# A convolution and MLP kernel whose exponential sums are kept and range-checked, with a looped general version behind a branch

## The chip, the cores and the metric

The kernel runs on one core of one Trainium2 chip. A core has five engines that run their own instruction lists and meet through semaphores: TensorE (PE in the profile; its weight loads are PEld), VectorE (DVE), ScalarE (ACT), GpSimd (POOL) and SyncE (SP), which here only issues DMAs. The metric is the device time of one execution in microseconds, lower is better.

## The reference

A dynamic convolution over seven taps, weighted by a softmax, followed by an MLP with the activation h - tanh(h):

```python
batch, seq, d_model = (8, 4096, 192); kernel_size = 7; n_heads = 8
...
w = weight_gen - np.max(weight_gen, axis=-1, keepdims=True)
w = np.exp(w)
w = w / (np.sum(w, axis=-1, keepdims=True) + 1e-09)
x_pad = np.concatenate([np.zeros((B, pad, D), dtype=np.float32), x], axis=1)
...
out = np.einsum('bshk,bskhg->bshg', w, x_unf)
...
h = x @ w_in
g = h - np.tanh(h)
return (g @ w_out).astype(np.float32)
```

`x` is drawn as 0.1 times a standard normal, `weight_gen` as 0.3 times one, `moe_w_in` and `moe_w_out` as normals over the square root of their first dimension.

## The kernel before

The 32,768 tokens are cut into 32 blocks (`NTOT`) of 1024 tokens (`TOK` = 128 partitions x `J` = 8). Everything is unrolled in Python; there is no loop or branch on the chip. A block `n` goes through these stages, several blocks being under way at once:

- `load_wg` and `load_x` (lines 116 and 126) fetch the tap weights and the tokens with their halo, on SyncE's queue.
- `softmax_exp` (167, ScalarE), `softmax_sum` (179, VectorE, in two halves of 32 columns), then the reciprocal (`softmax_norm`, 194; `softmax_recip`, 189) and the scaling (`scale`, 228). The kernel before takes exp of the raw weights, without subtracting the row maximum. Each block's 64 sums per partition live in a tile `zsum` of the pool `wgpool`, which has three buffers.
- `products` and `help` (261 and 243) multiply tokens and weights on GpSimd and VectorE; DMAs with accumulation sum some of the taps (`dma_sum`, 235).
- `conv_sums` and `conv_out` (367 and 395) sum the rest and transpose on TensorE into `convT`.
- `gemm1(n, f)` (422) makes, for each of 16 tiles `f` of the 2048 hidden columns, six matmuls into a PSUM tile `ph`; ScalarE takes tanh into `th` (line 440), VectorE subtracts into `gt` (line 441). `ph` comes from a PSUM pool with three buffers, which the transposes (`pc`) and the last block's outputs (`po2`) share.
- `out_stream` and `out_pairs` (481 and 525) feed the second matmul of earlier blocks between the first matmuls of this one, by hand-written counts (`STEADY`, 682, and others); `store_out` (508) copies a finished token tile out of PSUM and stores a block once its eight tiles are there.

The order on every engine is the order of the Python calls, as the whole body stands under `tc.manual_schedule()` (line 564). The main loop (707 to 768) runs `n` = 1 to 31 and `f` = 0 to 15. The exp of block `n + 4` is taken at f=1 of block `n`, its sums at f=1 and f=13, its reciprocal and scaling at f=14; from `n` = 28 on there is no such block.

After the loop comes the tail (770 to 774): the first half of `gemm2_last(0)`, the rest of `out_stream`, the second half, and then `gemm2_last(j)` (line 529) for the token tiles j = 1 to 7 of the last block. Each makes 32 matmuls into a `po2` tile, a ScalarE copy `ot` (551) and a VectorE add into `out_sb` (552). After every odd `j` SyncE stores two token tiles (554). The program then ends with a wait for all DMAs and a barrier of the engines, which the profile books under line 800.

Of the kernel before, what the change touches and what calls it, by code (L numbers as in the profile page):

```python
# [8 lines left out]
FP32 = mybir.dt.float32  # L9
BF16 = mybir.dt.bfloat16  # L10

ACT = mybir.ActivationFunctionType
AX = mybir.AxisListType


@with_exitstack
def kernel(
# [20 lines left out]
    JH = J // 2  # L38
    HT = TOK // 2
    NSB = S // TOK  # L40
    NTOT = B * NSB
    NFT = F // P
    NC = D // R
# [7 lines left out]
    HELP = {n: ((n - 2, 3),) for n in (4, 5, 6, 7, 8, 9, 10, 11, 12, 13, 14, 15, 16, 17, 18, 19, 20, 21, 22, 23, 24, 25, 26, 27, 28, 29, 30, 31)} | {9: ((7, 3), (6, 12)), 10: ((8, 3), (7, 12)), 11: ((9, 3), (8, 12)), 12: ((10, 3), (9, 12)), 13: ((11, 3), (10, 12)), 14: ((12, 3), (11, 12))}  # L51
    LAST_TAP = (4, 5, 6, 7, 8)
    X_LATE = ()
    ZERO_AT = 8
    PACE, PACED = None, ()
    SCALE_TWICE = True
# [24 lines left out]
    zero = const.tile([1, D], FP32, name="zero")  # L81
    nc.vector.memzero(zero[:])
    once = const.tile([P, 1], FP32, name="once")

    x_of = {}
    held = {}
# [2 lines left out]
    zsum_of = {}  # L89
    zr_of = {}  # L90
    wsm_of = {}
    prods_of = {}
    to_sum = {}
    conv_of = {}
# [99 lines left out]
    def softmax_norm(n, bank):  # L194

        wsm = softmax_tile()
        zr_v = bank[:, 512 - J * H : 512]
        nc.vector.reciprocal(zr_v, zsum_of[n][:])  # L198

        def finish():  # L200
            scale(nc.vector, wsm[:], e_of[n], zr_v)

        wsm_of[n] = (wsm, None, None, None)
        return finish

    def softmax_norm_ramp(n, bank):

        softmax_sum(n)
        wsm = softmax_tile()
        zr_v = bank[:, 512 - J * H : 512]  # L210
        nc.vector.reciprocal(zr_v, zsum_of[n][:])  # L211
# [14 lines left out]
        wsm_of[n] = (wsm, wsm_v, None, None)  # L226
# [298 lines left out]
    def out_pairs(m):  # L525
        for _ in range(m):
            next(pairs)

    def gemm2_last(j, f0=0, f1=NFT):
# [21 lines left out]
        nc.scalar.activation(out=ot[:], in_=po[:, 0, 0:D], func=ACT.Copy)  # L551
        nc.vector.tensor_add(out_sb[:, j, :], po[:, 1, 0:D], ot[:])
        if j % 2 == 1:
            nc.sync.dma_start(
                out=out[n * TOK : (n + 1) * TOK, :].rearrange("(p j) e -> p j e", p=P)[
                    :, j - 1 : j + 1, :
                ],
                in_=out_sb[:, j - 1 : j + 1, :],
            )
# [147 lines left out]
    for n in range(1, NTOT):  # L707
        more = n < NTOT - 1
        finish = []
        plan = FIRST if n == 1 else DOUBLE if n in DOUBLE_IN else APART if n in APART_IN else STEADY  # L710

        soft = [m for m in (n + 3 if n <= AHEAD else n + 4,) if m < NTOT]
        for f in range(NFT):
            ph = gemm1(n, f)
            if n == 1:
                if f == 1:
                    load_wg(5)
                if f == 5:
                    softmax_exp(4)
                steps = ((softmax_sum, 3), (softmax_recip, 3), (softmax_sum, 4))  # L720
                for at, (step, m, h) in zip(plan["sums"], [s + (h,) for s in steps for h in (0, 1)]):
                    if f == at:
                        step(m, h * JH, (h + 1) * JH)
                if f == 5:
                    wsm_of[3] = (softmax_tile(), None, e_of[3], zr_of[3])
                    rest = products(3)
            elif f == 1:
                if soft:
                    softmax_exp(soft[0])
                if n + 2 < NTOT:  # L730
                    rest = products(n + 2)
            if n == AHEAD and f == 4:
                softmax_exp(n + 4)
            if n > 1:
                for h, at in enumerate(plan["sums"]):
                    if soft and f == at:
                        softmax_sum(soft[0], h * JH, (h + 1) * JH)
            if n == AHEAD:
                for at, (step, h) in zip(EXTRA, [(s, h) for s in (softmax_sum, softmax_recip) for h in (0, 1)]):
                    if f == at:  # L740
                        step(n + 4, h * JH, (h + 1) * JH)
                if f == EXTRA[-1]:
                    wsm_of[n + 4] = (softmax_tile(), None, e_of[n + 4], zr_of[n + 4])
            for m in (n + 2, n + 3):
                if (n, f) in HELP.get(m, ()):
                    help(m, ph, J - 1 - HELP[m].index((n, f)))
            if n + 2 < NTOT and f == (9 if n == 1 else max([b for a, b in HELP.get(n + 2, ()) if a == n] + [3])):
                rest()
            if f == (9 if n == 1 else 1) and n > STORE_FIRST:
                loads(n)  # L750
            done = 0
            for chunks, at in sorted((((0, 1), plan["t2"]), ((2,), plan["t1"])), key=lambda c: c[1]):
                if more and at[0] == f:
                    out_pairs(at[1] - done)
# [12 lines left out]
            if f == (9 if n == 1 else 1) and n <= STORE_FIRST:  # L767
                loads(n)

    gemm2_last(0, 0, J)  # L770
    out_pairs(NFT)
    gemm2_last(0, J, NFT)
    for j in range(1, J):
        gemm2_last(j)


# [28 lines left out]
```

## Time and profile before

| What | Value |
|---|---|
| timed runs | 746.78 us median of 3 (745.8 to 747.22) |
| span of the profiled execution, which is a run of its own | 743.4 us |
| busy share: TensorE, its weight loads, VectorE, ScalarE, GpSimd | 97%, 75%, 92%, 86%, 88% |
| matmuls into `ph` (L427) | 3072, 415.1 us |
| second matmuls into `obank` (L495) | 7936, 408.0 us |
| subtractions `gt` (L441) | 512, 601.6 us, 1217 ns each |
| tanh `th` (L440) | 512, 512.1 us, 1025 ns each |
| sums `zsum` (L183) | 61, 23.6 us |
| final stores (L554) | 4 of 192 KB, 3.0 us from issue to landing (median) |

A group's busy time is the sum of its instructions' durations; matmuls overlap, so their sum can exceed the span. The idle time that the profile lists before an instruction is how long its engine did nothing, and the releaser is what it waited for. The chain of waits goes back from the last instruction to what released each one.

### The profile page before, as it was taken

Reading aid. Unit: us, or ns where it says so; the run is one execution under the profiler, and the core shown is the slowest. Engines: PE = TensorE matmul, PEld = TensorE weight load, DVE = VectorE, ACT = ScalarE, POOL = GpSimd, SP = SyncE. Lnnn points to the kernel's source line nnn. Section 1 sums busy time; section 2 is a strip of 40 time slices with the busy share of each in tenths; the row PEclk is TensorE's granted clock in tenths of the full one; section 3 lists DMA queues with packets and bytes.
Section 4 is the critical chain, followed back from the end, with each engine's and each line's share of the span. In section 5 each row is a group of like instructions: output and inputs, shape, how many; then the busy total and the mean of one; then the engine's idle time right before and its main releaser. Section 6 shows DMA issues by size and latency. Waiting matters only on the chain.

```text
span 743.4 us, 30037 instructions
## 1 busy us (share of the span) xinstructions
PE 722.3 (97%) x13616; PEld 556.5 (75%) x13616; DVE 687.4 (92%) x723; ACT 638.8 (86%) x872; POOL 654.5 (88%) x163
## 2 busy tenths in 40 slices
PE   3899999999999999999999999999999999999997
PEld 2477777778777777777777777777777777877777
DVE  7999899999999999999999999999999999988893
ACT  4888888888888888989889999898998989888882
POOL 7999999999999999999999999999999999991000
PEclk9899999999999999999999999999999999999999
DMA  8925367766567668878777977877887877776112
GB/s 236 245 46 161 135 172 185 195 179 149 124 183 184 183 185 224 210 199 203 166 202 209 236 186 204 178 195 205 221 209 195 192 181 194 193 149 110 45 45 86
DMA packets 34269, 130.06 MB, mean 175 GB/s; under 512 B 4591, under 2 KB 9439, under 8 KB 30174
## 3 DMA queue, kind: packets, MB, share of 16 engines
q0 software_dynamic: 19424, 51.12, 40.4%
q1 hardware_dynamic: 14718, 77.03, 27.6%
q8 instruction: 106, 1.74, 0.9%
q14 instruction: 21, 0.17, 0.1%
HBM read 54.52 MB, written 25.17 MB: 107 GB/s over the span
## 4 chain that ended last, share of the span: by engine, by line
PE 92%; DVE 5%; ACT 1%; issue 1%; DMA 1%; SPq 0%; DVEq 0%
PE ph L427 43%; PE obank L495 43%; PE pc L384 4%; DVE gt L441 3%; PE po L538 1%; ACT th L440 1%; DVE pa L299 1%; DMA wg_t<-in_weight_gen_dram 1%; DVE zsum L183 0%; SPq L134 0%; ACT convT L402 0%; DVE obank L211 0%; DVE pa L251 0%; DVE pb L299 0%; SPq L144 0%
## 5 line engine op out<-in xcount | busy, mean ns | idle before, releaser
L441 DVE TENSOR_TENSOR gt<-ph,th 128x1024 bf16<-128x1024 f32 x512 | 601.6, 1217 | 33.4 <-ACT th L440 23.2
L440 ACT ACTIVATE th<-ph 128x1024 f32<-128x1024 f32 x512 | 512.1, 1025 | 69.2 <-PE ph L427 60.3
L427 PE MATMUL ph<-convT,w_in 64*128 64x512 bf16 x3072 | 415.1, 379 | 5.3 <-DVE gt L441 3.3
L495 PEld LDWEIGHTS <-gt 64*128 64x128 bf16 x7936 | 355.6, 94 | 80.6 <-issue 6.3
L495 PE MATMUL obank<-w_out,gt 64*128 64x192 bf16 x7936 | 408.0, 243 | 0.9 <-issue 0.8
L299 POOL TENSOR_TENSOR pa<-x_t,wsm 128x2688 bf16<-128x2688 f32 (+3 forms) x68 | 338.9, 5232 | 0.2
L299 POOL TENSOR_TENSOR pb<-x_t,wsm 128x4608 bf16<-128x4608 f32 (+2 forms) x33 | 283.8, 8601 | 0.7 <-ACT wsm L221 0.5
L427 PEld LDWEIGHTS <-w_in 64*128 64x128 bf16 x3072 | 163.0, 94 | 86.0 <-issue 18.3
L514 ACT ACTIVATE out_sb<-obank 128x192 f32<-128x192 f32 x248 | 81.3, 328 | 11.2 <-PE obank L495 10.3
L410 ACT ACTIVATE convT<-pc 128x1024 bf16<-128x1024 f32 (+1 forms) x62 | 50.1, 810 | 2.9 <-PE pc L384 2.7
L236 POOL DMA_DIRECT2D pa<-pb x28 | 36.0, 1284 | 13.7 <-POOL pb L299 9.1
L384 PEld LDWEIGHTS <-pa 64*128 64x128 bf16 x2064 | 41.5, 100 | 6.8 <-DVE pa L299 1.1
L236 POOL DMA_DIRECT2D pa<-pa x21 | 34.7, 1651 | 9.6 <-DMA pa<-pb 8.9
L384 PE MATMUL pc<-ident,pa 64*128 64x64 bf16 x1968 | 41.2, 191 | 1.8 <-POOL pa L299 0.9
L183 DVE TENSOR_REDUCE zsum<-wg_t 128x32 f32<-128x224 f32 (+1 forms) x61 | 23.6, 387 | 2.9 <-ACT wg_t L169 2.9
L169 ACT ACTIVATE wg_t<-wg_t 128x448 f32<-128x448 f32 x32 | 18.2, 570 | 6.3 <-DMA wg_t<-in_weight_gen_dram 6.2
L251 DVE TENSOR_TENSOR pa<-x_t,ph 128x384 bf16<-128x384 f32 x34 | 18.8, 554 | 2.0 <-DVE ph L250 0.3
L229 DVE TENSOR_TENSOR wsm<-wg_t,pc 128x448 f32<-128x448 f32 x27 | 16.8, 621 | 2.5
L198 DVE RECIPROCAL pc<-zsum 128x64 f32<-128x64 f32 x27 | 14.9, 550 | 0.0
L384 PE MATMUL pc<-ident,pb 64*128 64x64 bf16 x216 | 4.9, 206 | 9.0 <-POOL pb L299 9.0
L384 PEld LDWEIGHTS <-pb 64*128 64x128 bf16 x288 | 6.3, 106 | 9.5 <-POOL pb L299 9.0
L538 PE MATMUL po<-w_out,gt 64*128 64x192 bf16 x256 | 11.2, 243 | 0.0
(27 smaller groups left out, 56.8 us busy)
## 6 DMA issues: line engine op xcount, KB each, us to landing
x_t<-in_x_dram SPq DMA_DIRECT2D x31, 1344.0 KB, 7.9
pa<-pb POOLq DMA_DIRECT2D x28, 1152.0 KB, 9.5
out_dram<-out_sb SPq DMA_DIRECT2D x31, 768.0 KB, 3.9
pa<-pa POOLq DMA_DIRECT2D x21, 768.0 KB, 7.2
wg_t<-in_weight_gen_dram SPq DMA_DIRECT2D x32, 224.0 KB, 7.1
x_t<-in_x_dram SPq DMA_DIRECT2D x1, 768.0 KB
w_out<-in_moe_w_out_dram POOLq DMA_DIRECT2D x1, 768.0 KB, 9.5
out_dram<-out_sb SPq DMA_DIRECT2D x4, 192.0 KB, 3.0
```

The source lines that it names most:

```text
L183: nc.vector.reduce_sum(out=zsum_of[n][:, j0 * H : j1 * H], in_=e_of[n][:, j0:j1].rearrange("p j h k -> p (j h) k"), axis=AX.X,)
L236: return nc.gpsimd.dma_start(out=out.rearrange("p k j d -> p k (j d)"), in_=in_.rearrange("p k j d -> p k (j d)"), accum_op=mybir.AluOpTyp ...
L251: nc.vector.tensor_mul(pa[:, 0:KH, j, :].rearrange("p k (h g) -> p k h g", h=H), bass.AP(tensor=x_v.tensor, offset=x_v.offset + j * D, ap= ...
L299: return eng.tensor_mul(prod(k0, k1)[:, :, j0:j1].rearrange("p k j (h g) -> p k (j h) g", h=H), bass.AP(tensor=x_v.tensor, offset=x_v.offs ...
L384: nc.tensor.matmul(pc[r][:, col : col + R] if home else pc[:, r, col : col + R], lhsT=prods[c][gi][r * R : (r + 1) * R, 2 * j : 2 * j + 2] ...
L410: last_conv[0] = nc.scalar.activation(out=out, in_=pc[:, :, 0:cols].rearrange("p r (cj t) -> p r cj t", t=R), func=ACT.Copy,)
L427: nc.tensor.matmul(ph[:, r, :], lhsT=w_in[r * R : (r + 1) * R, c, f * P : (f + 1) * P], rhs=convT[r * R : (r + 1) * R, c, :], start=(c == ...
L440: last_act[0] = nc.scalar.activation(out=th[:], in_=ph_f, func=ACT.Tanh)
L441: last_sub[0] = nc.vector.tensor_sub(gt[:], ph_f, th[:])
L495: mm = nc.tensor.matmul(po[:, 0:D], lhsT=g_of[n][f][r * R : (r + 1) * R, col : col + P], rhs=w_out[r * R : (r + 1) * R, f, :], start=(r == ...
L514: last_act[0] = nc.scalar.activation(out=out_sb[:, j, :], in_=po[:, 0:D], func=ACT.Copy)
L538: nc.tensor.matmul(po[:, r, 0:D], lhsT=g_of[n][f][r * R : (r + 1) * R, col : col + P], rhs=w_out[r * R : (r + 1) * R, f, :], start=(f == 0 ...
```

## The change

The sums of exponentials of all blocks are written side by side into one tile `zall` (128 x 2048) instead of into `zsum` buffers, and they are checked: their largest value must be at most 1e30 and their smallest at least 1e-18. The check is cut into eight pieces. Pieces 0 to 3 are reductions over halves of `zall`: the maximum of the first and second half at (n, f) = (28, 14) and (29, 14), the minimum of the first and second half at (30, 14) and (31, 8). After the loop, pieces 4 and 5 compare, piece 6 multiplies and moves the result of all partitions into one row by a DMA, and piece 7, ahead of token tile 4, reduces that row to one flag.

The flag is then loaded into a register of every engine, and where it is 0 the engines run a general version: loops on the chip over batch rows, blocks and hidden tiles that compute all outputs again, with the row maximum. The last of the four stores of the last block moves behind that branch. The four-store condition becomes the table `STORES`, whose last entry is added for the store at the end.

In the built program SyncE's list has, between the branch and the last store, eight waits for the eight semaphores of its DMAs with a jump, and then the 145 instructions of the general version, which the jump passes over. The general version has 171 instructions on TensorE, 122 on VectorE, 84 on ScalarE and 78 on GpSimd. VectorE, ScalarE, TensorE and GpSimd load the flag behind their last work, SyncE between the second and the third of the final stores.

```diff
+    STORES = {1: 0, 3: 2, 5: 4}
+    LAST_STORE = {7: 6}
+    SUM_MAX, SUM_MIN = 1e30, 1e-18
+    CHECK = {(28, 14): (0,), (29, 14): (1,), (30, 14): (2,), (31, 8): (3,)}
...
+    zall = const.tile([P, NTOT * J * H], FP32, name="zall")
+    ends = const.tile([P, 4], FP32, name="ends")
+    fine = const.tile([P, 2], FP32, name="fine")
+    fine_row = const.tile([1, 2 * P], FP32, name="fine_row")
+    flag = const.tile([1, 1], mybir.dt.int32, name="flag")
...
-            zsum_of[n] = wgpool.tile([P, J * H], FP32, name="zsum")
+            zsum_of[n] = zall[:, n * J * H : (n + 1) * J * H]
...
+    def sums_piece(i):
+
+        w = NTOT * J * H // 2
+        if i < 4:
+            op = ALU.max if i < 2 else ALU.min
+            nc.vector.tensor_reduce(ends[:, i : i + 1], zall[:, i % 2 * w : (i % 2 + 1) * w], AX.X, op)
+        elif i == 4:
+            nc.vector.tensor_scalar(ends[:, 0:2], ends[:, 0:2], SUM_MAX, None, op0=ALU.is_le)
+        elif i == 5:
+            nc.vector.tensor_scalar(ends[:, 2:4], ends[:, 2:4], SUM_MIN, None, op0=ALU.is_ge)
+        elif i == 6:
+            nc.vector.tensor_mul(fine[:], ends[:, 0:2], ends[:, 2:4])
+            nc.sync.dma_start(out=fine_row[:], in_=fine[:])
+        else:
+            nc.vector.tensor_reduce(flag[:], fine_row[:], AX.X, ALU.min)
...
-        if j % 2 == 1:
-            nc.sync.dma_start(
...
+        if j in STORES:
+            store_last(j)
...
-    ctx.enter_context(tc.manual_schedule())
+    sched = tc.manual_schedule()
+    sched.__enter__()
...
+            for piece in CHECK.get((n, f), ()):
+                sums_piece(piece)
...
+    for piece in (4, 5, 6):
+        sums_piece(piece)
     gemm2_last(0, 0, J)
     out_pairs(NFT)
     gemm2_last(0, J, NFT)
     for j in range(1, J):
+        if j == 4:
+            sums_piece(7)
         gemm2_last(j)
+    sched.__exit__(None, None, None)
...
+    def general(m, carry):
...
+        nc.vector.tensor_reduce(zr[:], e_v, AX.X, ALU.max)
+        nc.vector.tensor_sub(e_v, e_v, spread(zr[:]))
...
+        for k in range(K):
...
+        with tc.For_i(0, NFT) as f:
...
+    good = nc.values_load(flag[:], min_val=0, max_val=1)
+    with tc.If(good < 1, preferred_fallthrough_block=False):
+        with tc.For_i(0, B) as b:
...
+            with tc.For_i(0, NSB) as s:
+                general(b * NSB + s, carry)
+    STORES.update(LAST_STORE)
+    store_last(J - 1)
```

The inputs of the timed runs keep the sums within the two bounds.

More of the change, by code (lines that the diff above doesn't have):

```diff
@@ L13 @@
 AX = mybir.AxisListType
+ALU = mybir.AluOpType
 @with_exitstack
@@ L197, in softmax_norm @@
         zr_v = bank[:, 512 - J * H : 512]
-        nc.vector.reciprocal(zr_v, zsum_of[n][:])
+        nc.vector.reciprocal(zr_v, zsum_of[n])
         def finish():
@@ L210, in softmax_norm_ramp @@
         zr_v = bank[:, 512 - J * H : 512]
-        nc.vector.reciprocal(zr_v, zsum_of[n][:])
+        nc.vector.reciprocal(zr_v, zsum_of[n])
         if n == 2:
@@ L527, in out_pairs, with store_last @@
             next(pairs)
+    def store_last(j):
+        n = NTOT - 1
+        nc.sync.dma_start(
+            out=out[n * TOK : (n + 1) * TOK, :].rearrange("(p j) e -> p j e", p=P)[:, STORES[j] : j + 1, :],
+            in_=out_of[n][:, STORES[j] : j + 1, :],
+        )
     def gemm2_last(j, f0=0, f1=NFT):
@@ L552, in gemm2_last @@
         nc.vector.tensor_add(out_sb[:, j, :], po[:, 1, 0:D], ot[:])
-        if j % 2 == 1:
-            nc.sync.dma_start(
[L555 to L559, printed above, removed]
+        if j in STORES:
+            store_last(j)
     w_in = const.tile([P, NC, F], BF16, name="w_in")
     w_out = const.tile([P, NFT, D], BF16, name="w_out")
-    ctx.enter_context(tc.manual_schedule())
+    sched = tc.manual_schedule()
+    sched.__enter__()
     def load_w_out():
@@ L773, with rows, spread @@
     for j in range(1, J):
+        if j == 4:
+            sums_piece(7)
         gemm2_last(j)
+    sched.__exit__(None, None, None)
+    def general(m, carry):
+        x_t = xpool.tile([P, HALO + J, D], FP32, name="x_t")
+        def rows(p0, p1, r0, r1):
+            first = x.rearrange("b s d -> (b s) d")[bass.ds(m * TOK, 1)]
+            nc.sync.dma_start(
+                out=x_t[p0:p1, r0:r1, :],
+                in_=bass.AP(
+                    tensor=first.tensor,
+                    offset=first.offset + (p0 * J - HALO + r0) * D,
+                    ap=[[J * D, p1 - p0], [D, r1 - r0], [1, D]],
+                ),
+            )
+        rows(0, P, HALO, HALO + J)
+        rows(1, P, 0, HALO)
+        nc.sync.dma_start(out=x_t[0:1, 0:HALO, :], in_=carry[0:1, 0:HALO, :])
+        nc.sync.dma_start(out=carry[0:1, 0:HALO, :], in_=x_t[P - 1 : P, J : J + HALO, :])
+        e_t = wgpool.tile([P, J, H, K], FP32, name="wg_t")
+        nc.sync.dma_start(
+            out=e_t[:],
+            in_=weight_gen.rearrange("b s h k -> (b s) h k")[bass.ds(m * TOK, TOK)].rearrange(
+                "(p j) h k -> p j h k", p=P
+            ),
+        )
+        e_v = e_t[:].rearrange("p j h k -> p (j h) k")
+        zr = wgpool.tile([P, J * H], FP32, name="zr")
+        def spread(v):
+            return v.rearrange("p (n o) -> p n o", o=1).to_broadcast([P, J * H, K])
+        nc.vector.tensor_reduce(zr[:], e_v, AX.X, ALU.max)
+        nc.vector.tensor_sub(e_v, e_v, spread(zr[:]))
+        nc.scalar.activation(
+            out=e_t[:].rearrange("p j h k -> p (j h k)"),
+            in_=e_t[:].rearrange("p j h k -> p (j h k)"),
+            func=ACT.Exp,
+        )
+        nc.vector.reduce_sum(out=zr[:], in_=e_v, axis=AX.X)
+        nc.vector.reciprocal(zr[:], zr[:])
+        nc.vector.tensor_mul(e_v, e_v, spread(zr[:]))
+        total = papool.tile([P, J, D], FP32, name="total", tag="pa")
+        part = papool.tile([P, J, D], FP32, name="part", tag="pa")
+        summed = pbpool.tile([P, J, D], BF16, name="pb")
+        x_v = x_t[:]
+        for k in range(K):
+            to = total if k == 0 else part
+            nc.vector.tensor_mul(
+                to[:].rearrange("p j (h g) -> p (j h) g", h=H),
+                bass.AP(tensor=x_v.tensor, offset=x_v.offset + k * D, ap=[x_v.ap[0], [G, J * H], [1, G]]),
+                e_t[:].rearrange("p j h (k o) -> p k (j h) o", o=1)[:, k].to_broadcast([P, J * H, G]),
+            )
+            if k > 0:
+                nc.vector.tensor_add((summed if k == K - 1 else total)[:], total[:], part[:])
+        prods_of[NTOT] = [[summed[:]]] * NC
+        conv(NTOT, (0, 1), (2,))
+        convT = conv_of.pop(NTOT)
+        out_sb = opool.tile([P, J, D], FP32, name="out_sb")
+        nc.vector.memset(out_sb[:], 0.0)
+        with tc.For_i(0, NFT) as f:
+            w_f = tpool.tile([P, NC, P], BF16, name="w_f", tag="th")
+            nc.sync.dma_start(out=w_f[:], in_=w_in[:, :, bass.ds(f * P, P)])
+            w_o = tpool.tile([P, D], BF16, name="w_o", tag="th")
+            nc.sync.dma_start(out=w_o[:], in_=w_out[:, bass.ds(f, 1), :].rearrange("p o e -> p (o e)"))
+            ph = psum_h.tile([P, 2, HT], FP32, name="ph", tag="ph")
+            for c in range(NC):
+                for r in range(2):
+                    nc.tensor.matmul(
+                        ph[:, r, :],
+                        lhsT=w_f[r * R : (r + 1) * R, c, :],
+                        rhs=convT[r * R : (r + 1) * R, c, :],
+                        start=(c == 0),
+                        stop=(c == NC - 1),
+                    )
+            th = tpool.tile([P, TOK], FP32, name="th")
+            gt = gpool.tile([P, TOK], BF16, name="gt0", tag="gt0")
+            ph_f = ph[:].rearrange("p r t -> p (r t)")
+            nc.scalar.activation(out=th[:], in_=ph_f, func=ACT.Tanh)
+            nc.vector.tensor_sub(gt[:], ph_f, th[:])
+            for j in range(J):
+                po = psum_h.tile([P, 2, HT], FP32, name="po2", tag="ph")
+                col = (j % 2) * HT + (j // 2) * P
+                for r in range(2):
+                    nc.tensor.matmul(
+                        po[:, r, 0:D],
+                        lhsT=gt[r * R : (r + 1) * R, col : col + P],
+                        rhs=w_o[r * R : (r + 1) * R, :],
+                        start=True,
+                        stop=True,
+                    )
+                for r in range(2):
+                    nc.vector.tensor_add(out_sb[:, j, :], out_sb[:, j, :], po[:, r, 0:D])
+        nc.sync.dma_start(
+            out=out[bass.ds(m * TOK, TOK), :].rearrange("(p j) e -> p j e", p=P),
+            in_=out_sb[:],
+        )
+        (j,) = LAST_STORE
+        last = slice(LAST_STORE[j], j + 1)
+        nc.vector.tensor_copy(out_of[NTOT - 1][:, last, :], out_sb[:, last, :])
@@ L778 @@
+    good = nc.values_load(flag[:], min_val=0, max_val=1)
+    with tc.If(good < 1, preferred_fallthrough_block=False):
+        with tc.For_i(0, B) as b:
+            carry = xpool.tile([P, HALO + J, D], FP32, name="x_t")
+            nc.vector.memset(carry[0:1, 0:HALO, :], 0.0)
+            with tc.For_i(0, NSB) as s:
+                general(b * NSB + s, carry)
+    STORES.update(LAST_STORE)
+    store_last(J - 1)
 _INS = ['x', 'weight_gen', 'moe_w_in', 'moe_w_out']
```

## The prediction

> **What bounds the kernel now.** I read first the page's span and the chain of work that ended last, then VectorE's timeline over the last four blocks, then the tail.
>
> ```profile
> span 743.4 us, 30037 instructions
> ...
> PE 722.3 (97%) x13616; PEld 556.5 (75%) x13616; DVE 687.4 (92%) x723; ACT 638.8 (86%) x872; POOL 654.5 (88%) x163
> ...
> q8 instruction: 106, 1.74, 0.9%
> q14 instruction: 21, 0.17, 0.1%
> ...
> PE 92%; DVE 5%; ACT 1%; issue 1%; DMA 1%; SPq 0%; DVEq 0%
> ```
>
> (The q lines give packets, MB, and share of the DMA engines.) TensorE carries 92% of the chain, but VectorE (DVE) is 92% busy and close behind. The timeline of VectorE (start, duration, count, and the idle time before, with its releaser) shows where it is free:
>
> ```profile
> 660.85 1.22 DVE L441 TENSOR_TENSOR gt<-ph,th 128x1024 bf16<-128x1024 f32 x1 [0.69 <-ACT th L440]
> 662.47 1.23 DVE L441 TENSOR_TENSOR gt<-ph,th 128x1024 bf16<-128x1024 f32 x1 [0.40 <-ACT th L440]
> 664.35 2.36 DVE L441 TENSOR_TENSOR gt<-ph,th 128x1024 bf16<-128x1024 f32 x2 [0.66 <-PE ph L427]
> ...
> 718.49 7.18 DVE L441 TENSOR_TENSOR gt<-ph,th 128x1024 bf16<-128x1024 f32 x6 [0.25 <-ACT th L440]
> 725.96 2.53 DVE L441 TENSOR_TENSOR gt<-ph,th 128x1024 bf16<-128x1024 f32 x2 [0.29 <-ACT th L440]
> 730.73 0.36 DVE L552 TENSOR_TENSOR out_sb<-po,ot 128x192 f32<-128x192 f32 x1 [2.24 <-ACT ot L551]
> ...
> 739.97 0.36 DVE L552 TENSOR_TENSOR out_sb<-po,ot 128x192 f32<-128x192 f32 x1 [0.96 <-ACT ot L551]
> ```
>
> The 32 blocks have 16 subtractions each, so the last 16 before 730 are block 31, and the one at 718.49 is its f=8. From there to 725.7 VectorE has no gap. TensorE is tied to it: three `ph` tiles rotate, so `ph` of f=11 needs the subtraction of f=8 to have ended (718.49 + 1.22 = 719.71), and TensorE's timeline starts it 0.12 us later:
>
> ```profile
> 719.83 0.83 PE L427 MATMUL ph<-convT,w_in 64*128 64x512 bf16 x6
> ```
>
> At the end, SyncE (SP) issues the four partial stores, the third at 737.72 and the last right behind the final add (739.97 + 0.36 = 740.33); 743.4 less that is 3.1 us for landing and closing barrier. The waits of SyncE in that stretch show the landing:
>
> ```profile
> SPq L800 <- DMA out_dram<-out_sb: 1.1, 1, 1.1
> ```
>
> **The change part by part.**
>
> *Sums kept in `zall`.* The same reductions and reciprocals with another output address: in the built programs the lists of TensorE, ScalarE and GpSimd are equal up to the new tail, and VectorE's differs only by the added pieces. Cost 0; nothing has to hide it.
>
> *Four reductions over 128x1024 (pieces 0 to 3).* No such row exists. Reducing 128x224 takes 375 ns and 128x448 takes 614 (groups by form, L183): 239 ns for 224 more elements, 1.07 ns each. 1024 elements are then 614 + 576 x 1.07 = 1230 ns at most, and 1024 x 1.07 = 1090 without the part for many results; the 1024-wide subtraction takes 1217. I take 1.1 us of VectorE time, as this one writes a single column. In blocks 28 to 30 the piece stands behind f=14. There the softmax of a later block no longer runs, and VectorE idles 0.40 + 0.66 = 1.06 us before its next two works (rows at 662.47 and 664.35; the same at 684 and 706). So 1.06 of 1.1 is covered: 0.04 each, 0.1 for three. Without that cover each would cost its whole 1.1. In block 31 the piece stands behind f=8, in the run without gaps. The subtraction of f=9 comes 1.1 us late, `ph` of f=12 with it, and all that follows; the one gap left before the last subtraction is 0.29 us (row at 725.96). Cost 1.1 - 0.29 = 0.8. Sum 0.9. Bounds: 0, if TensorE had room after all; 0.94 + 3 x 0.17 = 1.5 at 1.23 us each.
>
> *Pieces 4 to 6 and their DMA.* Three instructions of 2 columns; the nearest row is the copy of 16 columns at 190 ns, so 0.6 us in the gap of 2.24 us before the first add. The DMA from 128 partitions into one row joins SyncE's queue ahead of the store of block 30, which waits for ScalarE until 730.04; a small strided load issues in 0.8 us (SyncE, 2.66 us) and the final stores land in up to 3.0. It is there by 734, and piece 7, ahead of the add of j=4, needs it at 735.1. Piece 7 reduces 256 elements: 136 + 256 x 1.07 = 0.4 us in a gap of 0.96. Cost 0; uncovered, it would be the excess over those gaps.
>
> *The register load and the branch.* Each of five engines loads the flag behind its last work. SyncE loads it between the second store (issued 735.1) and the third (737.7), 2.2 us of room behind piece 7. TensorE, ScalarE and GpSimd end sooner than VectorE; VectorE loads behind 740.33, with 2 us until the last landing. No row shows such a load; bounds 0 and 2.2, and I take it as hidden.
>
> *The last store behind the branch.* This is the new wait. SyncE's way past the branch waits for every outstanding DMA, so for the third store: it was issued at 737.72, and the fourth needs about 1.9 us by the row above (issue from 740.36 for 0.33, some small waits, then 1.1), which gives 739.6; the page's median of 3.0 gives 740.7. With 0.2 for the waits and the jump SyncE is at the last store at 739.8 and has 0.5 us until the final add is done. Behind the last store stands only the closing barrier, which everybody waits for. But the jump must pass the general version: 145 SyncE instructions in the built program. Instructions come by DMA: q8 moves 1.74 MB for TensorE's 27232, so 64 bytes each, and q14, for the others, 21 packets of 8.1 KB, so 128 instructions per packet. A jump of 145 skips more than one packet, so its target need not be loaded. A fetch then stands on the path. Its price is not in the trace: at least nothing (packet already there), at most the slowest such landing, 3.0 us plus 0.5 for a late third store. I take the last store's 1.9 less its issue, 1.5 us, and 0.5 of it is hidden: 1.0.
>
> [...]
>
> *Sum.* 0.9 + 1.0 = 1.9 us. The profiled execution goes from 743.4 to 745.3. The timed runs before have a median of 746.78, 3.4 us above that span, which I take as unchanged: 748.7 us.
>
> **The rivals.**
>
> A, not slower by more than can be told: the target of the jump is loaded. Then SyncE is ready at 739.8, before the final add, and only the reductions count: 746.78 + 0.9 = 747.7, +0.1%. For it: 0.5 us of room, and packets are plainly fetched ahead, since TensorE's 106 leave no gaps between its matmuls. Against: 145 is more than 128. It decides as long as fetch and jump together stay under some 1 us (0.9 + 0.6 = 1.5).
>
> B, several stalls: the third store lands at 740.7, a fetch costs 3.0, and VectorE's own load and jump (122 instructions) outlast the store. Worst sum 0.9 + 3.5 = 4.4, with 1.5 for the reductions 5.0; typical 4.0, so 750.8. For it: five engines each jump over 78 to 171 instructions, and the closing barrier takes the latest. Against: all but SyncE have 2 us or more.
>
> C, faster: separate places for the sums remove a reuse of three `zsum` buffers. The place would be the reductions at f=1; it would decide if they waited for an older reciprocal. Both stand on VectorE in order, and the row of L183 has no idle time before it, so the price is at most the 2.9 us of idle time that the page shows before L183, all at the ramp and from ScalarE: 743.9 at best.
>
> D, the general version runs: sums of seven exponentials of small weights lie far inside 1e-18 to 1e30. If it ran, 32 blocks with 7 products of 1.75 us each alone would add 392 us.
>
> **How the numbers follow.** Forecast 0.54, A 0.27, B 0.14, C 0.04, D 0.01. What a measurement can tell from no change is 0.2%, 1.5 us, so 748.3 is the border. Of the forecast's cases some 0.88 lie above it (0.475), with B, D and a little of A 0.63 for slower; the rest of the forecast and A make 0.33 for the same; C 0.04. The forecast's own range is 748.0 to 749.8. For 8 in 10 it reaches down to A less the spread of the runs (747.0) and up to B's typical case (751.0).
>
> **What would show it.** The reduction rows at 1.1 us, gaps behind f=14 filled, and the subtractions of block 31 some 1 us late from f=9; the final add 0.9 us later than 740.33; the last store's issue 1 us or more behind the final add, where now it follows at once; a packet of q14 between. If the store follows the add at once, A holds. If VectorE's or another engine's closing drain is last, B. I am wrong if the reductions cost more than 1.3 us each, since then the gaps behind f=14 no longer hold them, or if the register load takes more than 2 us.

## The result, and the profile after

The changed kernel takes 749.01 us (median of 4 runs, 748.39 to 750.31), the kernel before 746.29 us (4 runs, 745.68 to 747.22). The ratio is 1.0041, with a 95% interval of 1.0026 to 1.0057: slower by 2.7 us, as forecast in sign, with 748.7 us predicted. The profiled execution of the changed kernel timed 748.44 us and spans 746.7.

From the page of the changed kernel (span and instructions; busy time of each engine; the instruction queue that, by the prediction's count, serves the engines other than TensorE, in packets and MB; the chain that ended last):

```profile
span 746.7 us, 30082 instructions
...
PE 722.1 (97%) x13616; PEld 556.7 (75%) x13616; DVE 692.1 (93%) x731; ACT 638.7 (86%) x872; POOL 654.5 (88%) x163
...
q14 instruction: 25, 0.20, 0.1%
...
PE 90%; DVE 5%; ACT 1%; DMA 1%; issue 1%; DVEq 0%
```

TensorE, ScalarE and GpSimd work as long as before, within 0.2 us. VectorE has 4.7 us more (692.1 against 687.4), and that queue moved 25 packets where it was 21. VectorE's timeline (start, duration, what, count, idle time before and its releaser) shows where the four reductions fell:

```profile
661.53 1.23 DVE L467 TENSOR_TENSOR gt<-ph,th 128x1024 bf16<-128x1024 f32 x1 [0.96 <-ACT th L466]
662.67 1.21 DVE L204 TENSOR_REDUCE ends<-zall 128x1 f32<-128x1024 f32 x1
663.80 3.60 DVE L467 TENSOR_TENSOR gt<-ph,th 128x1024 bf16<-128x1024 f32 x3
...
719.18 1.22 DVE L467 TENSOR_TENSOR gt<-ph,th 128x1024 bf16<-128x1024 f32 x1 [0.25 <-ACT th L466]
720.33 1.21 DVE L204 TENSOR_REDUCE ends<-zall 128x1 f32<-128x1024 f32 x1
721.45 5.74 DVE L467 TENSOR_TENSOR gt<-ph,th 128x1024 bf16<-128x1024 f32 x5
727.45 2.53 DVE L467 TENSOR_TENSOR gt<-ph,th 128x1024 bf16<-128x1024 f32 x2 [0.27 <-ACT th L466]
...
741.47 0.36 DVE L585 TENSOR_TENSOR out_sb<-po,ot 128x192 f32<-128x192 f32 x1 [0.96 <-ACT ot L584]
```

Behind f=14 of block 28 the reduction stands where two gaps of 0.40 and 0.66 us were, and from there to f=8 of block 31 nothing is lost: 719.18 - 661.53 = 57.65 us, before 718.49 - 660.85 = 57.64. Behind f=8 it pushes what follows: the last subtraction ends 727.45 + 2.53 - 719.18 = 10.80 us after f=8 began, before it was 10.00. In the chain of waits that piece is a link of its own between two subtractions:

```profile
719.18 1.22 DVE gt L467
720.41 1.12 DVE ends L204
721.53 1.14 DVE gt L467
```

The tail: the final add ends at 741.47 + 0.36 = 741.83. SyncE's timeline has the last store, and its waits in that stretch (line waiting, what it waited for, us in total, times, longest) the landing and the closing barrier:

```profile
742.83 0.34 SPq L557 DMA_DIRECT2D out_dram<-out_sb  x1
```

```profile
SPq L950 <- DMA out_dram<-out_sb: 1.6, 1, 1.6
SPq L950 <- PEq L950: 1.0, 2, 0.8
```

The store is 1.00 us behind the add, where it was 0.03. From its issue to the end of the span it is 3.9 us, where it was 3.0; the wait for the landing alone grew from 1.1 to 1.6. The two spans then differ by these terms, each read from the rows of both:

| Stretch | before, us | after, us | difference |
|---|---|---|---|
| start to f=14 of block 28 (no piece has acted yet) | 660.85 | 661.53 | +0.7 |
| to f=8 of block 31 (three reductions) | 57.64 | 57.65 | 0.0 |
| to the end of the last subtraction (the fourth) | 10.00 | 10.80 | +0.8 |
| to the end of the final add | 11.84 | 11.85 | 0.0 |
| to the last store's issue | 0.03 | 1.00 | +1.0 |
| to the end of the span | 3.0 | 3.9 | +0.8 |
| sum | 743.4 | 746.7 | +3.3 |

The first term is no cost of the change: among thirteen profiled kernels that start lies anywhere between 660.85 and 662.29; the kernel before is at the low end, and so is `store_first`, an experiment below that has the whole change. The run's time is 1.7 to 1.9 us above its span in the executions that have both, the kernel before's among them, so its profiled execution stands for some 745.2 us and was one of the faster ones. The medians differ by 2.7 us, near the 2.6 that the three other terms add up to.

### The profile page after: what moved, and what is told of

Its sections match the earlier page's. It is cut to its first block, busy times and chain, and to the rows that moved or that the text cites. A ratio compares the mean times of both kernels' runs of the same rounds, so it can differ in the third digit from the quotient of the medians.

```text
span 746.7 us, 30082 instructions
## 1 busy us (share of the span) xinstructions
PE 722.1 (97%) x13616; PEld 556.7 (75%) x13616; DVE 692.1 (93%) x731; ACT 638.7 (86%) x872; POOL 654.5 (88%) x163
## 4 chain that ended last, share of the span: by engine, by line
PE 90%; DVE 5%; ACT 1%; DMA 1%; issue 1%; DVEq 0%
PE obank L521 43%; PE ph L453 43%; PE pc L410 4%; DVE gt L467 4%; PE po L571 1%; ACT th L466 1%; DMA x_t<-in_x_dram 1%; DVE pb L325 0%; DMA wg_t<-in_weight_gen_dram 0%; DVE pa L325 0%; DVE zall L193 0%; ACT convT L428 0%; DVE wsm L255 0%; ACT wg_t L179 0%; DVE obank L237 0%
## 5 line engine op out<-in xcount | busy, mean ns | idle before, releaser
L193 DVE TENSOR_REDUCE zall<-wg_t 128x32 f32<-128x224 f32 (+1 forms) x61 | 23.6, 387 | 2.9 <-ACT wg_t L179 2.9
L224 DVE RECIPROCAL pc<-zall 128x64 f32<-128x64 f32 x27 | 14.9, 550 | 0.0
```

What stands on the lines that cost most here:

```text
L193: nc.vector.reduce_sum(out=zsum_of[n][:, j0 * H : j1 * H], in_=e_of[n][:, j0:j1].rearrange("p j h k -> p (j h) k"), axis=AX.X,)
```

## The experiments

Eleven kernels ran, each beside the kernel before on the same chip. The theory that they began with: two costs, the fourth reduction in a stretch where VectorE has no gap, and a stall of SyncE at its jump over the general version, because the block of code with the jump's target has to be fetched. In the table, "f=8 to last" is from the start of the subtraction f=8 of block 31 to that of the last one, "add to store" from the end of the final add to the last store's issue, "jump" from SyncE's last branch to its next instruction, "packets" from the last store's issue to its last packet's end, and "to end" from its issue to the span's end, all in us.

| Kernel | Ratio to before, 95% | f=8 to last | add to store | jump | packets | to end |
|---|---|---|---|---|---|---|
| before | | 8.78 | 0.03 | none | 1.51 | 3.04 |
| changed | 1.0041 (1.0026 to 1.0057) | 9.58 | 1.01 | 1.43 | 2.06 | 3.85 |
| `sums_only` | 1.0001 (0.9992 to 1.0010) | 8.78 | 0.03 | none | 1.51 | 3.05 |
| `no_branch` | 1.0027 (1.0016 to 1.0037) | 9.58 | 0.03 | none | 1.48 | 3.27 |
| `no_branch_late` | 1.0002 (0.9991 to 1.0014) | 8.77 | 0.03 | none | 1.48 | 3.27 |
| `late_min` | 1.0036 (1.0022 to 1.0050) | 8.77 | 0.95 | 1.37 | 2.46 | 4.24 |
| `tiny_body` | 1.0023 (1.0014 to 1.0032) | 9.58 | 0.42 | 0.19 | 1.48 | 2.85 |
| `al50` | 1.0032 (1.0004 to 1.0059) | 9.58 | 0.42 | 0.44 | 2.40 | 4.23 |
| `al95` | 1.0044 (1.0028 to 1.0060) | 9.58 | 2.55 | 3.02 | 1.67 | 3.46 |
| `store_first` | 1.0055 (1.0040 to 1.0070) | 9.58 | 0.03 | 0.71 | 2.31 | 5.60 |
| `late_al50` | 1.0018 (1.0002 to 1.0033) | 8.77 | 0.42 | 0.44 | 2.34 | 4.14 |
| `early_load` | 1.0024 (1.0011 to 1.0037) | 8.77 | 0.09 | 0.44 | 2.54 | 4.32 |
| `small_early` | 0.9995 (0.9986 to 1.0004) | 8.78 | 0.08 | 0.19 | 1.48 | 2.85 |

**The sums alone (`sums_only`).** The kernel before with only the place of the sums changed:

```diff
+    zall = const.tile([P, NTOT * J * H], FP32, name="zall")
...
-            zsum_of[n] = wgpool.tile([P, J * H], FP32, name="zsum")
+            zsum_of[n] = zall[:, n * J * H : (n + 1) * J * H]
```

> The kernel before with its sums written to zall, without the check, the flag, the branch and the general version. Theory 1 (the cost is the one reduction in block 31 and SyncE's way past the branch): same as before, ratio 1.000 within 0.001. Rival R1 (the new place of the sums slows the body): some 0.7 us slower, ratio 1.001, since the changed kernel's subtractions stood 0.69 us later than before ahead of the first reduction's effect.

1.0001, within 0.1% either way. The separate places cost nothing and free nothing, so rival C of the prediction, a reuse of buffers that is no longer waited for, has no place.

**All pieces, no branch (`no_branch`).** The general version, the register load and the branch are left out, and the last store stands where it stood:

```diff
-    good = nc.values_load(flag[:], min_val=0, max_val=1)
-    with tc.If(good < 1, preferred_fallthrough_block=False):
...
     STORES.update(LAST_STORE)
     store_last(J - 1)
```

> All eight pieces of the check, but the flag is not read: no register load, no branch, no general version, the fourth store follows the third. Theory 1: only the reduction behind (31, 8) costs, final add 0.8 us later than in the kernel before once the drift of the body is taken off, store at once behind it, ratio 1.001. Rival R2 (the check costs all of the 2.7 us): ratio 1.0035 or more.

In the trace it does what was expected: 0.80 us between f=8 and the last subtraction, and the store at once behind the add. The time missed: 1.0027 where 0.8 us make 1.0011. It stayed open here whether the pieces cost something outside of these rows.

**The fourth reduction behind the last subtraction (`late_min`).**

```diff
-    CHECK = {(28, 14): (0,), (29, 14): (1,), (30, 14): (2,), (31, 8): (3,)}
+    CHECK = {(28, 14): (0,), (29, 14): (1,), (30, 14): (2,)}
...
-    for piece in (4, 5, 6):
+    for piece in (3, 4, 5, 6):
         sums_piece(piece)
```

> The changed kernel with piece 3 (the last minimum) moved from behind (31, 8) to behind the last subtraction, ahead of pieces 4 to 6, where VectorE had a gap of 2.24 us. Theory 1: 0.8 us faster than the changed kernel, the subtractions of block 31 keep their distance to those of block 30, and the way past the branch still costs 1.0; ratio to before about 1.003. Rival: the reduction costs as much there, in the gap ahead of the first add; ratio 1.004.

VectorE's timeline of this kernel has the eight last subtractions without a hole, as before, and the reduction and pieces 4 to 6 in the gap ahead of the first add, which still leaves 0.72 us:

```profile
719.39 7.18 DVE L467 TENSOR_TENSOR gt<-ph,th 128x1024 bf16<-128x1024 f32 x6 [0.25 <-ACT th L466]
726.85 2.53 DVE L467 TENSOR_TENSOR gt<-ph,th 128x1024 bf16<-128x1024 f32 x2 [0.28 <-ACT th L466]
729.30 1.21 DVE L204 TENSOR_REDUCE ends<-zall 128x1 f32<-128x1024 f32 x1
...
731.63 0.36 DVE L585 TENSOR_TENSOR out_sb<-po,ot 128x192 f32<-128x192 f32 x1 [0.72 <-ACT ot L584]
```

So the 0.80 us is the place, not the work: the same instruction 9 us later is free. The ratio of 1.0036 says less, since 0.8 us is 0.0011 and the interval is wider; half of what was won went again to a slower landing (2.46 us to the last packet, 2.06 in the changed kernel).

**The same without the branch (`no_branch_late`).** Both edits together.

> All eight pieces, the flag not read and no branch, and the fourth reduction behind the last subtraction, not behind f=8 of block 31; the general version is left out. Theory: piece by piece the checks then cost nothing that lies on the path, the last subtraction comes 8.78 us behind the one of f=8, the store 0.03 behind the final add, 1.5 us to its last packet; 1.000 (0.999 to 1.001). Rival, the run without the branch stood at 1.0027 where its trace explains 0.8 us, 1.0011, because the pieces cost something outside of these rows: then this run stands at 1.0015 to 1.002.

1.0002: all eight pieces are free in these places, and the rival falls that they cost something out of sight. The 1.0027 of `no_branch` then belongs to the place behind f=8 too or to the spread of its runs; the trace accounts for 0.0011 of it, and the rest isn't settled. The span from store to end is 3.27 in both, 0.2 more than before, without any branch; where that comes from is open as well. In both kernels a pause of SyncE at the end of a block of its code (0.38 to 0.39 us), read from the traces further below, stands earlier in the closing barrier than in the kernel before; whether that makes the 0.2 was not tested.

**No general version to jump over (`tiny_body`).** Flag, load and branch stay; the body is one instruction, and the general version is left out:

```diff
     with tc.If(good < 1, preferred_fallthrough_block=False):
-        with tc.For_i(0, B) as b:
...
-                general(b * NSB + s, carry)
+        nc.vector.memset(out_of[NTOT - 1][:, LAST_STORE[J - 1] : J, :], 0.0)
```

> The changed kernel with the general version left out: behind the branch stands one memset of the last output tile alone (it would zero that part if it ran). SyncE has no DMA waits and nothing to jump over. Theory 1 (the jump over 145 instructions costs): the fourth store is issued at most 0.2 us behind the final add instead of 1.0, the final landing takes 1.9 instead of 2.5 us; 1.0 to 1.6 us faster than the changed kernel, ratio to before about 1.001 to 1.002. Rival R3 (reading the flag and branching costs by itself): store still 1.0 us behind the add, ratio 1.004.

SyncE is past its branch in 0.19 us instead of 1.43, so the stall goes with the general version: with the code that is jumped over or with the eight waits, which this kernel lacks too. The next two runs part the two. Yet the store is not at 0.03 behind the add but at 0.42, which nothing in the prediction explains, and it lands faster again (1.48 us to the last packet, where the changed kernel has 2.06).

**The jump's target shifted (`al50`, `al95`).** If the stall is the fetch of a block of code, then where the blocks begin decides its length. One filler in SyncE's list, in the middle of block 30, shifts all that follows; the two kernels differ by 45 places and in nothing else:

```diff
             if f == (9 if n == 1 else 1) and n <= STORE_FIRST:
                 loads(n)
+            if (n, f) == (30, 4):
+                nc.sync.addr_align(128, offset=50, max_nops=0)
```

(`al95`: offset=95.) Counted in blocks of 128 instructions, the size of q14's packets (8192 bytes each in the traces, at the 64 for an instruction that the prediction worked out from q8's row), the first puts the target into the block next to the jump's own, the second into the block after that.

> The changed kernel, whole, with SyncE's list shifted when it is loaded (an alignment directive in block 30): its branch comes to stand some 65 instructions behind a boundary of 128 and the last store some 220 behind it, so in the next block of 128, and the boundary is crossed long before the branch. Theory F (the stall is the fetch of the block with the jump's target, not asked for until the branch): SyncE's time from its last branch to the wait ahead of the fourth store falls from 1.43 us to at most 0.3, the store follows the final add at once, 1.0 us faster than the changed kernel. Rival R4 (the length of the jump or the eight waits cost, whatever the place): 1.43 us as in the changed kernel.

> The same with the list shifted so that the branch stands some 110 behind a boundary and the last store some 265 behind it, so in the next block but one. Theory F: the block is not loaded when SyncE jumps, so the stall is 1.4 us or more, store 1.0 us or more behind the final add, no faster than the changed kernel. Rival R4: the same as in the run with the other shift.

The last store in SyncE's timeline, first of the kernel with the target in the next block, then of the other; the final add ended at 741.52 and 741.78:

```profile
741.94 0.34 SPq L557 DMA_DIRECT2D out_dram<-out_sb  x1
```

```profile
744.33 0.34 SPq L557 DMA_DIRECT2D out_dram<-out_sb  x1
```

From the branch to the next instruction it is 0.44 us in the one (0.3 at most was expected) and 3.02 in the other; the changed kernel, with 1.43, lies between, and one of its q14 packets starts at 741.2, just ahead of its branch at 741.31. The same instructions in other places cost from 0.44 to 3.02 us: the place of the target relative to these blocks decides, as the theory of a fetch has it, and the rival that SyncE waits for a landing falls, as all three waited for the same third store, and that wait was over before the branch.

Where the blocks end can be read from the traces as well. Counted in the instructions that the trace has, SyncE pauses for 0.38 to 0.39 us ahead of its 208th in each of the nine kernels whose list isn't shifted, whatever that instruction is. In the kernel before it pauses for 0.45 us ahead of its 80th, 128 earlier, between two issues that follow each other within 0.05 us the next time (start, duration):

```profile
261.56 0.33 SPq L134 DMA_DIRECT2D x_t<-in_x_dram  x1
262.34 0.97 SPq L120 DMA_DIRECT2D wg_t<-in_weight_gen_dram  x1
...
281.31 0.34 SPq L134 DMA_DIRECT2D x_t<-in_x_dram  x1
281.70 1.30 SPq L120 DMA_DIRECT2D wg_t<-in_weight_gen_dram  x1
```

In the changed kernel the pause (739.96 to 740.35) stands among the eight waits, four instructions ahead of the branch. The target, 145 instructions behind the branch, is thus in the next block there too, as in `al50`; but `al50` entered its block 52 us ahead of its branch, the changed kernel only 1 us. From leaving the old block to going on behind the jump it is 2.8 us in the changed kernel, 2.7 in `late_min` and 3.1 in `store_first`, and in `al95` 3.0 from the branch itself. These figures fit one reading, an estimate from them that no row shows by itself: the next block is asked for when a block is entered, or else by the jump, it takes some 3 us, and the stall is what is left of that at the branch. The 0.44 of `al50` is then little more than the pause of 0.38 to 0.45 us that was measured at a change of block without a jump. The packet at 741.2 took 0.31 us itself; what the rest of the 3 us is made of, and which of q14's packets are SyncE's, the traces don't show.

But `al50` gains only 0.6 us behind the add, not 1.0: again 0.42 remain. What SyncE waited for there, and the rows of the branch's line in this kernel, by queue (count, duration ns, first and last start):

```profile
SPq L557 <- DVEq L919: 0.5, 1, 0.5
```

```profile
L919 SPq COMPARE_BRANCH  x2: 33/39/45, 739.3 to 741.0; - x2
...
L919 DVEq COMPARE_BRANCH  x2: 51/53/55, 741.8 to 742.0; - x2
...
L919 DVEq EVENT_SEMAPHORE  x1: 21/21/21, 741.9 to 741.9; - x1
```

```profile
L918 DVEq TENSOR_LOAD <-flag x1: 537/537/537, 741.2 to 741.2; - x1
```

The store no longer waits for the add but for VectorE's semaphore, and in the path around the body VectorE raises it only behind its own branch. That branch needs the flag in VectorE's register, and the load of it, 0.54 us, is issued with the final add at 741.2. So 741.17 + 0.54 + the branch gives 741.9, 0.4 us behind the end of the add. In the changed kernel this wait is there too (its semaphore is raised at 742.2), hidden behind the longer stall.

**The store ahead of the branch (`store_first`).**

```diff
+    STORES.update(LAST_STORE)
+    store_last(J - 1)
     good = nc.values_load(flag[:], min_val=0, max_val=1)
...
-    STORES.update(LAST_STORE)
-    store_last(J - 1)
```

> The changed kernel with the fourth store ahead of the branch, behind the third (where the general version ran it would rewrite all outputs). SyncE then waits for the fourth store's landing before its jump, and the jump's stall stands behind it. Theory 1: the store follows the final add at once, 1.0 us gained, and the stall of some 1.4 us comes behind the landing, so 0.3 us slower to 0.3 faster than the changed kernel, ratio 1.004. Rival R5 (what matters is only when the last store is issued): 1.0 us faster, ratio 1.0025.

The store is at 0.03 again, but the profiled execution ends 5.63 us behind the final add, where it was 4.85 in the changed kernel; the intervals of the two times overlap. SyncE's way past the branch waits for every DMA, now the fourth store too, which has landed at 743.97; branch at 744.12, next instruction 0.71 later, and the closing barrier behind that. The stall is not saved, it comes after the landing instead of beside it. It is shorter than 1.43 us, which fits the reading above: the branch now comes 2.37 us behind the start of SyncE's pause and not 1.35.

**Both costs mended (`late_al50`).** The edits of `late_min` and `al50` together.

> Piece 3 behind the last subtraction and SyncE's list shifted as in the first run of this call. Theory 1 with F: both costs are gone, 1.8 us faster than the changed kernel and up to 2.4 if the final landing falls to 1.9 us, ratio to before 1.000 to 1.001. Rivals: R4 1.003, and 1.002 if the landing keeps its 0.6 us.

1.0018, the least of the kernels that keep range check, branch and general version, but above the 1.000 to 1.001 expected: the 0.42 is still there, and the landing is no faster (2.34 us to the last packet).

**The flag loaded earlier (`early_load`).** `late_al50`, with the load ahead of the last copy and add:

```diff
         if f1 < NFT:
             return
+        if j == J - 1:
+            good[0] = nc.values_load(flag[:], min_val=0, max_val=1)
...
-    good = nc.values_load(flag[:], min_val=0, max_val=1)
-    with tc.If(good < 1, preferred_fallthrough_block=False):
+    with tc.If(good[0] < 1, preferred_fallthrough_block=False):
```

> The fourth reduction stands behind the last subtraction, SyncE's list is aligned as in the run with both mended, and the flag is now loaded into the engines' registers ahead of the last copy and the last add; the comparison and the branch stay behind them. Theory: in the run with both mended the store still stood 0.42 us behind the final add because VectorE raises the semaphore that the store waits for only behind its own load of the flag (0.54 us) and its branch, begun at the add. With the load in the idle 0.96 us ahead of the add, the store's distance falls from 0.42 to about 0.1 us and the time by 0.3 us, to 747.4 (1.0014 to 1.0018). Rival, SyncE's own way past the branch holds the store: the distance stays at 0.4. Rival, the load delays the last add: the add then comes over 1.6 us behind the one before it, where it is 1.32 now, and the store is close behind it.

The load and the semaphore on VectorE, and its last two adds:

```profile
L582 DVEq TENSOR_LOAD <-flag x1: 537/537/537, 739.6 to 739.6; - x1
```

```profile
L921 DVEq EVENT_SEMAPHORE  x1: 21/21/21, 741.3 to 741.3; - x1
```

```profile
739.59 0.36 DVE L588 TENSOR_TENSOR out_sb<-po,ot 128x192 f32<-128x192 f32 x1 [0.96 <-ACT ot L587]
740.91 0.36 DVE L588 TENSOR_TENSOR out_sb<-po,ot 128x192 f32<-128x192 f32 x1 [0.96 <-ACTq L921]
```

The adds keep their distance of 1.32 us, so the load delays nothing, and the store stands 0.09 us behind the add: the second wait is shown, and gone. The time did not follow: 1.0024 against 1.0018, intervals that overlap. Of the 0.33 us won at the issue the two profiled executions show 0.18 given back behind it (4.32 us to the end, 4.14 in `late_al50`), as the last packet now takes 2.54 us; the remaining 0.15 is less than the times can tell.

**The same without a general version (`small_early`).** The body of `tiny_body` in `early_load`, without the filler; the general version is left out.

> Fourth reduction behind the last subtraction, flag loaded ahead of the last copy and add, branch kept, and the general version replaced by one memset, so that its computation is left out and no engine has code to fetch at the end. Theory: what is left of the change in the run with the early load (1.0024) is the last store's slow landing, 2.5 us from issue to the last packet where 1.5 is usual, because the engines fetch code in that stretch. Without the general version the landing is back at 1.5 us, the store 0.1 us behind the add, and the time is that of the kernel before within 0.5 us: 1.0005 (0.9995 to 1.0015). Rival, the branch and the load themselves hold the store or the closing barrier: the landing stays over 2 us, or the span ends over 3.4 us behind the last store, and the ratio stays at 1.002.

0.9995: with nothing to jump over, range check, load and branch cost nothing that can be measured. The transfers around the last store, first of `early_load` (740.5 to 748), then of `small_early` (740 to 746), by queue with packets, MB and share:

```profile
q1 hardware_dynamic: 144, 0.20, 8.3%
q14 instruction: 5, 0.04, 1.9%
q8 instruction: 1, 0.02, 0.9%
```

```profile
q1 hardware_dynamic: 144, 0.20, 8.8%
q14 instruction: 1, 0.01, 0.5%
```

Both move the same 144 packets of the last store. With a general version five packets of code on q14 and one on q8 (16.4 KB, 1.1 us), by the prediction's count TensorE's, come beside them, four of the six between 741.7 and 743.3, while the store is issued at 741.36 and its packets run from 742.2 to 743.9; the ends of the last dozen are spread over 0.45 us. Without it the last dozen end within 0.1 us, the last at 742.54. `al95` fits: its store is issued at 744.33, when four such packets are through and one is to come, and it takes 1.67. That the general version lengthens the landing is shown by the two pairs (2.06 to 1.48, 2.54 to 1.48) and by the whole table: 1.67 to 2.54 in the seven kernels with it, 1.48 to 1.51 in the six without. That the code packets do it by taking turns with the store's on the DMA engines is an inference from these rows; no run separated it from other effects of the jumps.

No version that keeps the general version beat the kernel before.

## Why the prediction was right, and where it was not

- *Separate places for the sums, 0.* Right (`sums_only`, 1.0001).
- *Three reductions behind f=14, 0.1 in all.* 0.01 measured. The cover was worked out from the gaps of 0.40 and 0.66 us, and held although a reduction took 1.21 us, not 1.1: from its start to the next instruction's it is 1.13. The bound of 1230 ns was right for the duration, the 1.1 for the time that it takes from VectorE.
- *The fourth, 0.8.* 0.80 measured, by the chain that was named, and 0 when moved behind the last subtraction.
- *Pieces 4 to 7 and their DMA, 0.* Right (`no_branch_late`, 1.0002).
- *The register load, "I take it as hidden".* This step failed, though the changed kernel does not show it. The load was weighed against the last landing and against SyncE's own room; that VectorE's way around the branch raises the semaphore which the store waits for was overlooked. It was worth 0.4 us where the stall was shorter (the store 0.42 us behind the add in `al50`, `late_al50` and `tiny_body`, 0.09 in `early_load`).
- *The last store behind the branch, 1.0.* 0.98 measured, as a stall at the jump, where it was placed. The stall, taken as 1.5 us, is 1.43; SyncE was at its branch 0.5 us ahead of the add's end (741.31 and 741.83). The 0.2 for the waits and the jump stood in no row of the kernel before; in the changed kernel the branch comes 0.25 us behind the end of SyncE's last wait (741.06), and in `tiny_body` SyncE was past its branch in 0.19. That a stall of that size came out is partly luck: 1.5 us was taken from a store's landing, 0.44 or 3.02 us were as possible, and only the position in the code decided. The argument that 145 is more than 128 did not settle it: the target lay in the next block, and by the reading above its fetch was under way when SyncE jumped. Rival A's condition, a loaded target, is by that reading met in `al50`, and even there the store waits 0.42.
- *Behind the last store "only the closing barrier".* A term is missing from the sum here: 0.8 us in the profiled executions, 0.56 of it a slower landing. It is why 2.6 us were found where 1.9 were summed.
- *The base.* The sum was set on a median of 746.78; with the fourth run the kernel before stands at 746.29. The missing term and the lower base nearly cancel in the time of 748.7, so that it came within 0.3 us is luck. The 3.4 us between the span of 743.4 and the median was no offset of each run either: a run's time is 1.7 to 1.9 us above its own span, and the profiled execution was a fast one.
- Rival B had several stalls in it and a third store landing late. The third store was in time; what it got right is that the general version costs more than SyncE's stall, not by an engine that outlasts the store but, as far as the rows of the landing go, by code packets beside it (2.06 us to the last packet, 1.48 in `tiny_body`). C fell with `sums_only`, and D did not occur.

## What to carry to other kernels

A check in the body costs what its place costs: the same 1.2 us reduction was free in a gap and 0.8 us on a full engine, so look for the gap ahead of the final adds before splitting the work. The rarely taken branch ahead of the last store was priced here by three things beside the comparison: the stall at the jump over the general version (0.44 to 3.02 us by its place), the register load on VectorE, whose semaphore the store waits for (0.42 us behind the add, 0.09 with an earlier load), and the slower landing of the store with code traffic around it (1.67 to 2.54 us to its last packet, 1.48 to 1.51 without the general version). The first two were mended by the position of the code and an earlier load: in `al50` the branch stands in a block that was entered 52 us before, and its target in the next. The third went where the general version was left out (1.48 us in `small_early`); a smaller one was not tried.

## What the runs showed of the hardware that was not expected

- A jump over 145 instructions cost SyncE 0.44 (`al50`), 1.43 (changed) or 3.02 us (`al95`), by its place relative to blocks of 128 instructions and by how long before it SyncE had entered its block; with hardly anything to jump over, 0.19. Going on into the next block without a jump cost 0.38 to 0.45 us.
- A load of one 4-byte flag from the on-chip memory into a register took 0.46 to 0.56 us on each of the five engines where it stood behind their work; it can lie beside the engine's running instruction (VectorE's started at 741.5 in the changed kernel, its last add at 741.47).
- A store of 192 KB whose packets end 1.5 us behind its issue took 1.7 to 2.5 us where packets of the instruction queues ran around it, in `early_load` three packets of 8.2 KB and one of 16.4 KB under the store itself.
- The start to f=14 of block 28, the same work in all kernels, varied over 1.4 us from one profiled execution to the next. A single pair of spans can't show an effect of that size; the distances between rows near the change can.
